# Cutting eight output stores by partitions: half-row stores of the first column half in two or three transfers each

## The chip, the cores and the metric

The kernel runs on one core of a Trainium2 chip. The metric is the device time of one execution in microseconds. The kernel before takes 368.6 us, the median of two runs (367.9 and 369.3).

## The reference, cut to what matters

Attention with a sigmoid in place of the softmax over 8 batches, 12 heads, 448 positions and head size 64; its output, as 3584 rows of 768 columns, goes through a soft mixture of experts with 8 experts of 4 slots each. All data is float32.

```python
attn = sigmoid(q @ k.T / sqrt(64) - log(448)) @ v        # per batch and head
x = attn.transpose(0, 2, 1, 3).reshape(3584, 768)
logits = x @ phi                                          # 3584 x 32
d = softmax over the 3584 rows;  slot_input = d.T @ x     # 32 x 768
h = relu(slot_input[e] @ w1[e]);  slot_out[e] = h @ w2[e] # w1: 768 x 1024, w2: 1024 x 768
c = softmax over the 32 slots;   out = c @ slot_out       # 3584 x 768
```

The weights w1 and w2 are 25 MB each, the output is 11 MB.

## The kernel before, in words

**Attention, to about 290 us.** Pairs of heads pass through TensorE (scores, then the product with v), with the sigmoid on ScalarE and the transposes on VectorE. Beside it SyncE loads q, k, v and the expert weights. The weights go into a ring of SBUF tiles (`ring_tile`, `load`, lines 116 to 173): a load waits until the tile's last reader is done, and the last weights of all are issued by SyncE between 296 and 313 us.

**Experts, to about 340 us.** `w1_part` and `h_part` (lines 716 to 736) work through w1, expert by expert. Then `w2_step` (lines 834 to 845) works through w2 in two column halves of 384 columns (`HALF`): the sixteen steps of half 0 first (lines 861 to 866), then the sixteen steps of half 1 (lines 870 to 880). Each step waits for the weights that it multiplies. `spread_sum` makes the 128-row operand `st` of one half, from which the output tiles of that half can be made.

**Output.** An output tile is 128 rows by 384 columns: `out_tile` (lines 787 to 790) is one matmul of the combine weights with `st` and one copy from PSUM to SBUF, on ScalarE for even tiles and VectorE for odd ones. `out_half(m, hf)` (lines 792 to 797) makes two such tiles, of row blocks m and m+1 and column half hf, side by side in one SBUF tile, and stores them in one transfer of 384 KB: each of the 128 partitions holds two runs of 384 floats (1536 bytes), which go to two rows of the output, 128 rows apart.

The order of the stores, all of them issued by SyncE, is fixed by the program. Eight calls of `out_half(m, 0)`, for m = 0, 2, ..., 14, stand between the w2 steps of half 1, one after each of the steps 4 to 11 (lines 879 and 880). After the last w2 step and its `spread_sum` come two stores of whole rows of one row block (`out_rows`, lines 882 and 883, 384 KB each), three of whole rows of two, four and four row blocks (`out_many`, lines 885 to 887, 768, 1536 and 1536 KB), and last the eight stores `out_half(m, 1)` (lines 889 and 890). The prediction calls the first eight the first-half stores, and the last eight the second-half stores.

Every engine executes its instructions in the order in which they are written (the program fixes the schedule of all five). SyncE's instructions from 296 us on are DMA issues alone: the last weight loads, then the stores. Ahead of each issue stands a wait for the data and for a DMA semaphore. The tile framework hands out the DMA semaphores by itself; the code names none.

Of the kernel before, what the change touches and what calls it, by code (L numbers as in the profile page):

```python
# [18 lines left out]
P = 128  # L19
# [10 lines left out]
HALF = DM // 2  # L30
# [26 lines left out]
ROWS = 128  # L57
NG = B * S // ROWS
NH = 16
LAG_T = 3  # L60
C4W = NBK * 4 * NSLOT
NR = 2
# [8 lines left out]
def soft_moe_attention(ctx: ExitStack, tc: tile.TileContext, qk, v, vl, first, phi, w, wq, w8, wz, cst, out):  # L71
    nc = tc.nc
# [43 lines left out]
    def ring_tile(size=1):  # L116
        while state["used"] + size > state["room"]:
            pool, n, used, room = slots[state["ring"]]
            state.update(ring=state["ring"] + 1, used=used, room=room)
            if pool == "wa":  # L120
                pool = wpa.tile([P, room * UNIT], F32, name=f"wa{n}")
            state["tile"] = pool
        t = state["tile"][:, state["used"] * UNIT:(state["used"] + size) * UNIT]
        state["used"] += size
        return t
# [67 lines left out]
    with ExitStack() as actx:  # L193
# [377 lines left out]
        for r in range(NP // 2):  # L571
            p = 2 * r
# [184 lines left out]
    def combine_split(n):  # L757
        lt, k = pieces[n][:2]
        c4 = wc_last[:, n % 3 * C4W:(n % 3 + 1) * C4W].rearrange("p (k a z s) -> p k a z s", k=NBK, a=2, z=2)
        nc.vector.tensor_copy(c4[:, 0:k, 0, 0, :], lt)  # L760
        nc.vector.tensor_tensor(
            out=c4[:, 0:k, 0, 1, :], in0=lt, in1=c4[:, 0:k, 0, 0, :].bitcast(F32), op=ALU.subtract)
        nc.scalar.copy(c4[:, 0:k, 1, :, :], c4[:, 0:k, 0, :, :].bitcast(F32))
        return c4

    def combine_turn(n, c4):
        pt = pt_tile()
        _, k, t0, nt = pieces[n]
        for c in range(k):
            w = min(P, nt - c * P)  # L770
            nc.tensor.transpose(
                out=pt[:, c * P:c * P + w], in_=c4[0:w, c].rearrange("p a z s -> p (a z s)").bitcast(F32),
                identity=csb[0:w, 0:w])
        at0 = t0
        while at0 < t0 + nt:
            i, m = divmod(at0, UNIT)
            w = min(UNIT - m, t0 + nt - at0)
            if m == 0:
                cts[i] = big[:, i * UNIT:(i + 1) * UNIT]
            nc.scalar.copy(cts[i][:, m:m + w], pt[:, at0 - t0:at0 - t0 + w])  # L780
            at0 += w
# [5 lines left out]
    def out_tile(ov, m, hf, k, t=0, n=1):  # L787
        pf = ps_t.tile([P, 512], F32, name="pt") if k % 2 else av_tile("av0")
        nc.tensor.matmul(pf[:, 0:HALF], ct_of(m, t, n), sts[hf], start=True, stop=True)  # L789
        (nc.scalar.copy, nc.vector.tensor_copy)[k % 2](ov, pf[:, 0:HALF])  # L790

    def out_half(m, hf):
        ov = ring_tile().rearrange("p (j c) -> p j c", j=2)
        for j in range(2):
            out_tile(ov[:, j, :], m + j, hf, j)
        nc.sync.dma_start(
            out[m * ROWS:(m + 2) * ROWS, hf * HALF:(hf + 1) * HALF].rearrange("(j p) c -> p j c", p=P), ov)

    def out_rows(m):
        ov = ring_tile().rearrange("p (j c) -> p j c", j=2)  # L800
        for hf in range(2):
            out_tile(ov[:, hf, :], m, hf, hf)
        nc.sync.dma_start(out[m * ROWS:(m + 1) * ROWS, :].rearrange("p (j c) -> p j c", j=2), ov)
# [10 lines left out]
    def gather(po):  # L814
        so = sb2.tile([P, HALF], F32, name="tmp")
        nc.scalar.copy(so[:], po[:, 0:HALF])
        return so

    def spread_sum(so, cuts=(0, HALF)):
        if sts:  # L820
            st = wc_last[:, 0:HALF]
        else:
            st = sb2.tile([P, HALF], F32R, name="st")[:]
        parts = list(zip(cuts, cuts[1:]))
        prs = [ps_t.tile([P, 512], F32, name="pt") if k else av_tile("av1") for k in range(len(parts))]
        for pr, (c0, c1) in zip(prs, parts):
            nc.tensor.matmul(pr[:, 0:c1 - c0], rep, so[:, c0:c1], start=True, stop=True)
        for pr, (c0, c1) in zip(prs, parts):
            (nc.scalar.copy if len(parts) > 1 else nc.vector.tensor_copy)(st[:, c0:c1], pr[:, 0:c1 - c0])
            nc.vector.tensor_tensor(  # L830
                out=st[64:128, c0:c1], in0=pr[64:128, 0:c1 - c0], in1=st[64:128, c0:c1].bitcast(F32), op=ALU.subtract)
        sts.append(st)

    def w2_step(po, hf, n):
        e, g = divmod(n, 2)
        h = hw[e % 2]
        if g == 0:
            o = NSLOT - SPE
            nc.gpsimd.tensor_copy(
                h[:, o:o + NFC * NSLOT].rearrange("p (f s) -> p f s", f=NFC)[:, :, 0:SPE], hc[:, e])  # L840
        for fl in range(4):
            k = (4 * g + fl) * NSLOT + NSLOT - SPE - SPE * e
            nc.tensor.matmul(  # L843
                po[32 * fl:32 * fl + 32, 0:HALF], h[:, k:k + NSLOT], w2_chunk(hf, e, g, fl),
                start=(n == 0), stop=(n == 2 * E - 1))
# [15 lines left out]
    for e in range(E):  # L861
        w2_step(po, 0, 2 * e)
        w2_step(po, 0, 2 * e + 1)
        if e >= LAG_T:
            combine_turn(e - LAG_T, c4s[e - LAG_T])
        c4s[e] = combine_split(e)
# [3 lines left out]
    for n in range(2 * E):  # L870
        w2_step(po, 1, n)
        if n == 1:
            spread_sum(so)
        if n < LAG_T:
            combine_turn(E - LAG_T + n, c4s[E - LAG_T + n])
            if n == LAG_T - 1:
                sctx.close()
                ps_t = ctx.enter_context(tc.tile_pool(name="ps_t", bufs=4, space=PSUM, reuse_waits="tile"))
        if 4 <= n < 4 + NH // 2:
            out_half(2 * (n - 4), 0)  # L880
    spread_sum(gather(po), (0, HALF // 2, HALF))
    for m in range(NH, NH + NR):
        out_rows(m)
    m = NH + NR
    for n in MANY:
        out_many(m, n)
        m += n
    assert m == NG
    for m in range(0, NH, 2):
        out_half(m, 1)  # L890
# [51 lines left out]
```

## Time and profile before

| | |
|---|---|
| median of two runs | 368.6 us |
| the profiled execution's own time | 368.86 us |
| its span, first to last instruction | 367.0 us |
| TensorE busy | 346.7 us, 94% of the span |
| VectorE, ScalarE, GpSimd busy | 66%, 61%, 3% |
| mean granted TensorE clock | 0.987 |
| bytes moved by DMA | 95.21 MB, mean 259 GB/s |
| output stores | 384 KB x18, 768 KB x1, 1536 KB x2 |

The shares are means over the whole span. The profile also cuts the span in 40 slices of 9.2 us and gives for each how busy an engine was and how many GB/s the DMA engines moved; the last slices are the ones in which the output is stored. The DMA share is the mean over the core's 16 DMA engines of the time that their packets took; since packets overlap a little it can stand some per cent above 1.

### The profile page before, as it was taken

Reading aid. Unit: us, or ns where it says so; the run is one execution under the profiler, and the core shown is the slowest. Engines: PE = TensorE matmul, PEld = TensorE weight load, DVE = VectorE, ACT = ScalarE, POOL = GpSimd, SP = SyncE. Lnnn points to the kernel's source line nnn. Section 1 sums busy time; section 2 is a strip of 40 time slices with the busy share of each in tenths; the row PEclk is TensorE's granted clock in tenths of the full one; section 3 lists DMA queues with packets and bytes.
Section 4 is the critical chain, followed back from the end, with each engine's and each line's share of the span. In section 5 each row is a group of like instructions: output and inputs, shape, how many; then the busy total and the mean of one; then the engine's idle time right before and its main releaser. Section 6 shows DMA issues by size and latency. Waiting matters only on the chain.

```text
span 367.0 us, 10400 instructions
## 1 busy us (share of the span) xinstructions
PE 346.7 (94%) x4341; PEld 158.7 (43%) x4341; DVE 242.7 (66%) x621; ACT 222.2 (61%) x307; POOL 10.1 (3%) x45
## 2 busy tenths in 40 slices
PE   9999999999999999999999999999999999897840
PEld 5333333544444446444444644464446554332620
DVE  0148829797795886859948695878956676232650
ACT  4777777677777774777777387747583123432640
POOL 1000000000000000000000000010003001000000
PEclk9999999999999999999999999999999999999995
DMA  7566666565677663666576378829989999999998
GB/s 256 184 219 197 200 225 189 174 210 160 229 227 212 200 197 110 212 198 211 196 230 187 121 256 262 283 59 372 318 300 332 421 436 425 415 422 406 399 419 305
DMA packets 34639, 95.21 MB, mean 259 GB/s; under 512 B 3616, under 2 KB 17184, under 8 KB 33184
## 3 DMA queue, kind: packets, MB, share of 16 engines
q1 hardware_dynamic: 34016, 92.58, 71.5%
q10 hardware_dynamic: 576, 1.97, 1.5%
q8 instruction: 34, 0.56, 0.6%
q14 instruction: 13, 0.11, 0.1%
HBM read 83.53 MB, written 11.01 MB: 258 GB/s over the span
## 4 chain that ended last, share of the span: by engine, by line
PE 85%; DMA 9%; DVE 2%; ACT 0%; issue 0%; ACTq 0%; DVEq 0%
PE sc L282 35%; PE av L327 34%; DMA wpe<-in_wq_dram 9%; PE av L189 6%; PE sc L449 3%; PE sc L387 2%; DVE wa L790 1%; PE av L789 1%; PE av L843 1%; PE sc L369 1%; PE av L567 1%; PE pt L789 1%; PE av L302 1%; PE av L449 0%; PE av L282 0%
## 5 line engine op out<-in xcount | busy, mean ns | idle before, releaser
L294 ACT ACTIVATE big<-sc,sm 128x896 f32<-128x896 f32 x167 | 167.7, 1007 | 77.2 <-PE sc L282 74.2
L327 PE MATMUL av<-big 64*64 64x448 f32 x1260 | 146.7, 536 | 0.0
L282 PE MATMUL sc<-big 64*64 64x448 f32 x896 | 111.3, 537 | 0.0
L327 PEld LDWEIGHTS av<-big 64*64 64x64 f32 x1260 | 47.5, 133 | 71.2 <-issue 68.9
L351 DVE STREAM_TRANSPOSE wa<-wpe 32x384 f32<-32x384 f32 (+5 forms) x144 | 58.0, 403 | 2.2
L282 PEld LDWEIGHTS sc<-big 64*64 64x64 f32 x896 | 35.5, 133 | 49.7 <-issue 39.9
L282 PE MATMUL sc<-wk 64*64 64x448 f32 x420 | 55.8, 537 | 0.0
L351 DVE STREAM_TRANSPOSE wa<-xy 32x192 f32<-32x192 f32 (+3 forms) x96 | 33.1, 345 | 1.6
L334 DVE TENSOR_TENSOR wpe<-wpe,av 128x448 f32<-128x448 f32 x18 | 11.2, 621 | 31.8 <-PE av L327 20.5
L282 PEld LDWEIGHTS sc<-wk 64*64 64x64 f32 x420 | 17.4, 133 | 22.3 <-issue 19.2
L351 DVE STREAM_TRANSPOSE wa<-wpx 32x288 f32<-32x288 f32 (+1 forms) x48 | 25.0, 520 | 0.8
L843 PE MATMUL av<-wa,hw 128*32 128x384 f32 x208 | 20.3, 493 | 2.7 <-DMA wa<-in_w_dram 1.6
L334 DVE TENSOR_TENSOR wpx<-wpx,av 128x448 f32<-128x448 f32 x15 | 9.3, 621 | 18.3 <-PE av L327 16.0
L189 PE MATMUL av<-wa,phi 128*32 128x256 f32 x312 | 18.2, 381 | 0.6 <-DVE phi L531 0.4
L790 DVE COPY wa<-pt 128x384 f32<-128x384 f32 x23 | 11.8, 554 | 4.5 <-PE pt L789 4.1
L790 ACT COPY wa<-av 128x384 f32<-128x384 f32 x23 | 10.7, 481 | 5.9 <-PE av L789 5.3
L334 DVE TENSOR_TENSOR xy<-xy,av 128x448 f32<-128x448 f32 x14 | 8.7, 621 | 8.3 <-ACT xy L330 6.6
L189 PEld LDWEIGHTS av<-wa,phi 128*32 128x32 f32 x312 | 9.6, 110 | 8.0 <-DVE phi L531 0.8
L736 ACT COPY t<-tmp 128x32 f32<-128x32 f32 x8 | 1.7, 218 | 18.3 <-DVE tmp L734 13.6
L351 DVE STREAM_TRANSPOSE wpe<-xy 32x256 f32<-32x256 f32 (+3 forms) x32 | 11.0, 345 | 0.5
L351 DVE STREAM_TRANSPOSE wpy<-wpx 32x288 f32<-32x288 f32 (+3 forms) x22 | 9.3, 424 | 0.4
L330 ACT COPY wpe<-av 128x448 f32<-128x448 f32 x18 | 9.4, 524 | 0.0
(191 smaller groups left out, 281.9 us busy)
## 6 DMA issues: line engine op xcount, KB each, us to landing
wa<-in_w_dram SPq DMA_DIRECT2D x52, 384.0 KB, 4.1
big<-in_qk_dram SPq DMA_DIRECT2D x32, 448.0 KB, 3.6
wa<-in_wq_dram SPq DMA_DIRECT2D x6, 1536.0 KB, 29.1
wa<-in_w_dram SPq DMA_DIRECT2D x3, 3072.0 KB, 20.8
big<-in_v_dram SPq DMA_DIRECT2D x45, 192.0 KB, 2.5
wk<-in_qk_dram SPq DMA_DIRECT2D x15, 448.0 KB, 3.3
out_dram<-wa SPq DMA_DIRECT2D x13, 384.0 KB, 7.4
out_dram<-wa SPq DMA_DIRECT2D x2, 1536.0 KB, 7.5
```

The costliest lines, as they stand in the source:

```text
L189: nc.tensor.matmul(ph[32 * j:32 * j + 32, 0:256], phi_sb[:, kc, :], wt, start=(kc == 0), stop=(kc == NKC - 1))
L282: nc.tensor.matmul(sc[h][64 * t:64 * t + 64, 0:S], qkts[pt][r, S + k0:S + k0 + 64], qkts[pt][r, 0:S], start=True, stop=True)
L294: nc.scalar.activation(att, tile2[:, :, 0:S], AF.Sigmoid, bias=nbias, scale=QSCALE)
L327: nc.tensor.matmul(o[t][r, 0:S], w, att[row, h, :], start=start, stop=stop)
L330: nc.scalar.copy(x_of(p), avs[p][1][:, 0:S])
L334: nc.vector.tensor_tensor(out=x_of(p), in0=x_of(p), in1=av[0][:, 0:S], op=ALU.add)
L351: nc.vector.transpose(y[32 * g:32 * g + 32, k0:k0 + n, c0:c0 + m, BLK * a:BLK * a + BLK], src)
L387: nc.tensor.matmul(lg[32 * j:32 * j + 32, BLK * c0[j]:BLK * (c0[j] + n)], phi_sb[:, hp, :], blocks(x, j if x is xa else (j + 2) % 4, n), s ...
L449: nc.tensor.matmul(sls[t][32 * a:32 * a + 32, BLK * k0:BLK * k1], zt[:, c * BLK:(c + 1) * BLK], y_of(t, gi, c)[:, k0:k1, BLK * a:BLK * a + ...
L789: nc.tensor.matmul(pf[:, 0:HALF], ct_of(m, t, n), sts[hf], start=True, stop=True)
L790: (nc.scalar.copy, nc.vector.tensor_copy)[k % 2](ov, pf[:, 0:HALF])
L843: nc.tensor.matmul(po[32 * fl:32 * fl + 32, 0:HALF], h[:, k:k + NSLOT], w2_chunk(hf, e, g, fl), start=(n == 0), stop=(n == 2 * E - 1))
```

## The change

`out_half` cuts its store along the partitions. A table gives the cuts for the first-half stores; a store that is not in the table goes out in one transfer as before. The tiles, the copies that fill them, the bytes stored and the order of the stores stay the same. Twelve transfers are added: the eight first-half stores become twenty.

```diff
+CUTS = {
+    (0, 0): (0, 120, 125, P), (2, 0): (0, 120, 127, P), (4, 0): (0, 120, 126, P), (6, 0): (0, 120, 124, P),
+    (8, 0): (0, 98, P), (10, 0): (0, 104, P), (12, 0): (0, 72, P), (14, 0): (0, 88, P)}
@@ out_half
-        nc.sync.dma_start(
-            out[m * ROWS:(m + 2) * ROWS, hf * HALF:(hf + 1) * HALF].rearrange("(j p) c -> p j c", p=P), ov)
+        rows = out[m * ROWS:(m + 2) * ROWS, hf * HALF:(hf + 1) * HALF].rearrange("(j p) c -> p j c", p=P)
+        cuts = CUTS.get((m, hf), (0, P))
+        for a, b in zip(cuts, cuts[1:]):
+            nc.sync.dma_start(rows[a:b], ov[a:b])
```

The pieces, in partitions, are 120+5+3, 120+7+1, 120+6+2, 120+4+4, 98+30, 104+24, 72+56 and 88+40.

## Rows read from the trace of the kernel before

**Rows 1.** The page: span, and DMA share (tenths) and rate in 40 slices.
```profile
span 367.0 us, 10400 instructions
...
DMA  7566666565677663666576378829989999999998
GB/s 256 184 219 197 200 225 189 174 210 160 229 227 212 200 197 110 212 198 211 196 230 187 121 256 262 283 59 372 318 300 332 421 436 425 415 422 406 399 419 305
```
**Rows 2.** The chain of waits from 300 us on: start, duration, what.
```profile
305.72 33.14 DMA wpe<-in_wq_dram
...
351.75 2.10 DVE wa L790 x4
```
**Rows 3.** Stretches: busy us (and count) of PE, PEld, DVE, ACT, POOL, PEclk, DMA share, GB/s.
```profile
339.00:344.00 5.00, 3.72 (x26) 2.13 (x26) 1.35 (x4) 1.99 (x6) 0.00 (x0) 1.00 1.07 397
344.00:347.00 3.00, 2.96 (x11) 2.69 (x12) 2.86 (x6) 2.48 (x6) 0.00 (x0) 1.00 1.03 392
347.00:350.00 3.00, 3.00 (x13) 2.40 (x12) 2.78 (x6) 2.62 (x6) 0.00 (x0) 1.00 1.06 438
...
354.00:364.00 10.00, 0.00 (x0) 0.00 (x0) 0.00 (x0) 0.00 (x0) 0.00 (x0) 0.67 1.02 390
364.00:365.00 1.00, 0.00 (x0) 0.00 (x0) 0.00 (x0) 0.00 (x0) 0.00 (x0) 0.50 0.99 364
365.00:365.50 0.50, 0.00 (x0) 0.00 (x0) 0.00 (x0) 0.00 (x0) 0.00 (x0) 0.50 0.26 95
```
**Rows 4.** SyncE's DMA issues in order of time: start, first to last end, what, count.
```profile
296.05 4.32 SPq L171 DMA_DIRECT2D wa<-in_wq_dram  x4
300.87 5.17 SPq L171 DMA_DIRECT2D wpe<-in_wq_dram  x2
313.03 0.33 SPq L139 DMA_DIRECT2D wpx<-in_wz_dram  x1
326.65 0.40 SPq L796 DMA_DIRECT2D out_dram<-wpx  x1
327.97 8.13 SPq L796 DMA_DIRECT2D out_dram<-wpy  x4
337.05 3.05 SPq L796 DMA_DIRECT2D out_dram<-wa  x3
343.97 1.12 SPq L803 DMA_DIRECT2D out_dram<-wa  x2
```
**Rows 5.** SyncE's waits, 326 to 367 us: total, times, longest.
```profile
SPq L938 <- DMA out_dram<-wa: 5.0, 1, 5.0
...
SPq L803 <- DVE wa L790: 3.8, 1, 3.8
SPq L796 <- DMA wa<-in_wq_dram: 3.0, 2, 1.7
SPq L796 <- DMA wpe<-in_wq_dram: 2.3, 2, 1.4
```
**Rows 6.** The load issued at 298.6: issue ns, start, us to landing.
```profile
L171 SPq DMA_DIRECT2D wa<-in_wq_dram x1: 328/328/328, 298.6 to 298.6; - x1
...
DMA to landing us min/median/max: 32.7/32.7/32.7
```
**Rows 7.** SyncE's issue of the fourth first-half store: start, duration.
```profile
331.45 2.38 SPq L796 DMA_DIRECT2D out_dram<-wpy  x1
```
**Rows 8.** The first of the first-half stores: issue ns, start, us to landing.
```profile
L796 SPq DMA_DIRECT2D out_dram<-wpx x1: 399/399/399, 326.6 to 326.6; - x1
...
DMA to landing us min/median/max: 13.7/13.7/13.7
```
**Rows 9.** The last of the first-half stores: issue ns, start, us to landing.
```profile
L796 SPq DMA_DIRECT2D out_dram<-wa x1: 643/643/643, 339.5 to 339.5; - x1
...
DMA to landing us min/median/max: 7.7/7.7/7.7
```
**Rows 10.** The page's DMA issues, the smallest of many: count, KB each, us to landing.
```profile
big<-in_vl_dram SPq DMA_DIRECT2D x23, 64.0 KB, 2.0
```

## The prediction, made before the changed kernel ran

> **What bounds the kernel now.** The stores belong to the last tenth of the span, so I read the page's slices first, then the chain of waits from 300 us on, then short stretches of the tail, then SyncE's own queue. In the slices the DMA share stands at nine tenths or more from about 290 us to the end, at 400 to 436 GB/s [rows 1]: the last weights and then the output go through full DMA engines. The chain says the same of the weights: 33.14 us of it are one load, issued at 305.72 and landed at 338.86 [rows 2]. After that the chain runs through the copies, which end at 351.75 + 2.10 = 353.85 us [rows 2]; it follows engines and does not see that the stores go on for 12 us after the last copy. The stretches do: from 354 to 364 no engine computes and the DMA share is 1.02 [rows 3]. SyncE's wait for the last store is its longest in this time, 5.0 us [rows 5].
>
> So the end is set by how long the DMA engines need for their bytes once the weights are in. What matters is the slowest of the sixteen. The share is 0.99 in 364 to 365 and 0.26 in the half microsecond after it [rows 3]: all sixteen run dry within about 1 us of each other. None is a straggler that would gain from a smaller part, and none has more than some half microsecond of room for a larger one.
>
> SyncE's queue holds a second limit. The fourth first-half store is issued at 331.45 [rows 7], just when a load issued at 298.6 lands, 298.6 + 32.7 = 331.3 [rows 6]. Counted through the issues, that load is the eighth transfer before it [rows 4]. Four first-half stores wait for a load in this way [rows 5]. I read it as eight DMA semaphores in rotation: a transfer goes out when the eighth one before it has landed.
>
> **The change, part by part.** Bytes, tiles, copies and matmuls stay. Three things change: how the first-half stores lie on the sixteen DMA engines, how many transfers pass through SyncE, and which landing each waits for.
>
> *The load of the engines.* A whole half-row store is 128 partitions, 8 for each of 16 engines. Its price comes from the stretch that holds nothing but such stores: 393,216 bytes at 390 GB/s [rows 3] are 1.01 us, so one partition costs the engine that carries it 0.126 us. No row shows a transfer of other than 128 partitions, so I bound the new distribution. One end: the pieces spread as evenly as before, and no engine gets more; 0 us. The other end: a piece is cut into equal shares of whole partitions, on as many engines as divide it, always from the same first engine on. Then that engine carries 8+1+1, 8+1+1, 8+1+1, 8+1+1, 7+2, 8+2, 6+4 and 8+4 partitions, 81 in place of 64: 17 x 0.126 = 2.14 us more. The sixteenth carries none of the eight stores and is 64 x 0.126 = 8.1 us ahead, which helps nobody, as every later store again needs all sixteen. I take the second end, because equal shares are the nearest to the one thing that is seen, sixteen engines that end together [rows 3]. A row shows no engine's number, so whether the first engines are the early or the late ones within that 1 us is open: 2.14 less up to 1 is the lower end of this case.
>
> The Trainium skill, page "DMA: Bandwidth & Descriptors", section "Why a DMA increments its semaphore by 16 and not by 1", states such a rule: the number of engines is the largest one up to 16 that divides the partitions, and they are the lowest-numbered. No run here shows it yet; by it the count is the same 81.
>
> *Twelve more issues.* An issue takes 0.40 us where nothing holds it [rows 8], so twelve are 4.8 us of SyncE. Nothing that is computed waits for SyncE here. Between the eighth first-half store, out at 337.05 + 3.05 = 340.10, and the first whole-row store at 343.97 [rows 4] it waits 3.8 us for VectorE's copy [rows 5], and it waits ahead of that too. The issues alone cost 0; without that cover they would cost 4.8.
>
> *The eight semaphores.* This is the added wait. Before, all eight stores were out at 340.1 us. After, the first eight transfers are only stores 1 and 2 and two pieces of store 3; pieces 4 to 8 wait for the loads for which stores 4 to 8 waited, so the eighth piece goes out at about 339.5. The ninth waits for the first piece, which lands where the first store did, at 326.6 + 13.7 = 340.3 [rows 8]. Pieces 9 to 16 leave as 1 to 8 land, until about 343. A transfer needs at least some 2.0 us from issue to landing [rows 10], so pieces 17 to 20 and the whole-row stores behind them go out from about 345 on: the first whole-row store is piece 21 and leaves between 345 and 347.5 in place of 343.97. What hides this is the engines' backlog: before, the last first-half store landed at 339.5 + 7.7 = 347.2 [rows 9], and on the engine with 81 partitions that becomes 349.3. The engine that sets the end thus still has work when the late store arrives. Ends: 0 (fully covered) and 3.5 us (the whole delay is idle time of the slowest engine). I take 0.3, near the covered end, because the backlog of 347.2 lies so close to 347.5.
>
> *Sum.* 2.14 + 0 + 0.3 = 2.4 us on the profiled execution's 368.86 gives 371.3. The median of the runs is 0.26 below that execution; I give **371.2 us**, 0.7% slower, which counts as no change: about 2%, 7.4 us, is what a measurement of this kernel can tell from none.
>
> **The rivals.**
>
> *Pieces of part of the partitions move more slowly* (slower). The price above assumes that an engine moves its partitions at the usual rate whichever they are. If the engines that share a piece get into each other's way at the SBUF side, each of the eight stores takes longer. At half the rate they take 8 x 1.01 = 8.1 us more, 368.86 + 2.14 + 8.1 = 379; at two thirds of the rate 4 us more, 375. It decides, that is passes 2%, from about 5 us on, 0.65 us a store. For it: all traffic here is at 390 to 438 GB/s whatever is moved [rows 3], as if something common limits it. Against it: the engines read the pieces out of step, since a piece waits in each engine's queue behind other work. The Trainium skill, page "SBUF — State Buffer", section "Door 1: The DMA port swizzle (why [64,N] ≈ [32,N])", speaks for it: 64 partitions in a row reach half of the 16 ports and get about half the bandwidth. By it the first part of 72+56 or 88+40, more than half of which lies in the lower 64 partitions, would be slow. No run here shows it.
>
> *Nothing happens* (no change). The pieces spread evenly all the same, or the first engines are ahead by as much as they get. Then only covered issues are added: 368.2 to 369.8. For it: between 344 and 347 the rate falls to 392 from the 438 of the next stretch [rows 3], so some engines have idle time there. At (438 - 392)/438 of 3 us that is 0.3 us each on average, too little for 2.14. That the change does not do what it says, because pieces land on all sixteen engines, is this case too.
>
> *A small gain.* The engines relieved are the late ones, and those loaded have room. The ends lie within 1 us [rows 3], so the gain is at most half of that and the 0.3 us above: 0.8, or 367.8 us. Against it: the 17 extra partitions alone are twice the whole spread.
>
> **How the numbers follow.** Chances: the forecast, 369.8 to 373, 0.53; slower pieces, 373 to 380, 0.21, of which half is above 376; nothing happens, 0.20; a small gain, 0.06. For the range I leave out the gain and the part of the second case above 376.5: 368.2 to 376.5. Faster by over 2% would need 361.2 us, which no case reaches, so 0.01 for what I have not thought of; slower by over 2% gets the upper half of the slow case, 0.11; within 2% the remaining 0.88.
>
> **What would show it.** Right: in the last 2 to 3 us before the last landing the DMA share falls in steps well below 1, as lightly loaded engines finish first; the first whole-row store leaves at 345 to 347.5 us; and SyncE's waits ahead of the cut stores and of the first whole-row store now name stores. If the sixteen still end within 1 us, the shares are not as I count them. If the rate of 339 to 344 us stands far below 397 GB/s [rows 3] while many engines have work, the slow pieces are at work. The prediction is wrong if the stores' queue is kept empty by the semaphores for several microseconds, or if the weights' last landing, at 338.86 [rows 2], moves.

## The result, and the profile after

The changed kernel takes 373.86 us, the median of two runs (373.59 and 374.12), against 368.6 us before: the ratio is 1.0138 with a 95% interval of 1.0113 to 1.0163, so 4.2 to 6.0 us slower. The forecast was 371.2 us in a range of 368.2 to 376.5. The sign and the range held; the loss is twice the forecast 2.6 us, and it lies where the prediction had put one of its rivals (373 to 380).

The page first: the span is 4.8 us longer than before.

```profile
span 371.8 us, 10412 instructions
...
DMA packets 34705, 95.21 MB, mean 256 GB/s; under 512 B 3682, under 2 KB 17250, under 8 KB 33250
```

The same line of the page before:

```profile
DMA packets 34639, 95.21 MB, mean 259 GB/s; under 512 B 3616, under 2 KB 17184, under 8 KB 33184
```

The bytes are the same. The packets under 512 B are 3682 where the page before has 3616. They count the engines that a transfer uses, one small packet for each: 3616 is 226 x 16, one for each of 16 engines of 226 transfers. The eight whole stores had 8 x 16 = 128. Equal whole shares of the pieces (15+5+3, 15+7+1, and so on) make 193; the piece of one partition, which holds two runs, can go on two engines and makes it 194. 194 - 128 = 66 is the measured difference. So the pieces do leave engines out, as the prediction took it, and no piece of 120 is on sixteen engines.

The weights' last landing, in the chain of waits (start, duration, what), is where it was, 338.67 for 338.86 [rows 2]:

```profile
305.51 33.16 DMA wpe<-in_wq_dram
```

The stretches (columns as in [rows 3]) show where the time went:

```profile
339.00:344.00 5.00, 3.68 (x27) 2.12 (x20) 1.54 (x4) 2.18 (x6) 0.00 (x0) 1.00 0.80 234
344.00:347.00 3.00, 3.00 (x12) 2.75 (x12) 2.84 (x7) 2.49 (x6) 0.00 (x0) 1.00 0.79 232
347.00:350.00 3.00, 3.00 (x13) 2.41 (x13) 2.85 (x6) 2.52 (x7) 0.00 (x0) 1.00 0.74 218
350.00:354.00 4.00, 3.07 (x13) 1.61 (x12) 3.67 (x8) 3.05 (x7) 0.00 (x0) 1.00 1.03 399
...
364.00:368.00 4.00, 0.00 (x0) 0.00 (x0) 0.00 (x0) 0.00 (x0) 0.00 (x0) 0.50 1.04 369
...
369.00:370.00 1.00, 0.00 (x0) 0.00 (x0) 0.00 (x0) 0.00 (x0) 0.00 (x0) 0.50 0.99 353
370.00:371.00 1.00, 0.00 (x0) 0.00 (x0) 0.00 (x0) 0.00 (x0) 0.00 (x0) 0.50 0.23 83
```

Between 339 and 350 us the DMA engines move 234, 232 and 218 GB/s where they moved 397, 392 and 438 [rows 3]. That is (163 x 5 + 160 x 3 + 220 x 3) KB = 1.96 MB that is missing at 350 us, 4.9 us at 400 GB/s: as much as the whole loss. Two things make up the low rate. The share is 0.74 to 0.80, so engines stand idle a fifth to a quarter of the time. And a busy engine moves less: 234/0.80 = 293 GB/s for each full share, against 397/1.07 = 371 before. From 350 us on the engines are full again, and they end together: 0.99, then 0.23. The steps at the end that the prediction asked for are not there.

The trace's records of single packets (one run of bytes that one engine moves) size both. The half-row runs are packets of 1536 bytes. Of those that begin between 339 and 350 us the median takes 65 ns in both kernels, but 350 of 1632 take 100 ns or more in the changed kernel, 4 of 1709 before. Per engine, what packets take beyond the median of their size in the kernel before adds up to 1.8 us, against 0.1, and the packets keep an engine busy for 8.6 us, against 11.4 (more than the 11 us of the stretch, because packets overlap). So of the 4.9 us some 2.8 us are idle time and some 1.7 us are slow packets: a fifth of the packets are much slower, not all of them a little.

SyncE's issues in order of time (columns as in [rows 4]) and three of its waits (as in [rows 5]):

```profile
327.97 1.07 SPq L802 DMA_DIRECT2D out_dram<-wpx  x3
331.25 11.77 SPq L802 DMA_DIRECT2D out_dram<-wpy  x11
343.14 4.50 SPq L802 DMA_DIRECT2D out_dram<-wa  x6
347.74 1.92 SPq L808 DMA_DIRECT2D out_dram<-wa  x2
349.76 3.33 SPq L815 DMA_DIRECT2D out_dram<-wa  x3
```

```profile
SPq L802 <- DMA wpe<-in_wq_dram: 2.8, 2, 1.6
SPq L802 <- ACT wa L793: 2.0, 4, 0.8
SPq L802 <- DMA out_dram<-wpx: 0.7, 1, 0.7
```

The first whole-row store (L808) leaves at 347.74 in place of 343.97 [rows 4]. Only 0.7 us of this is a wait for a store. The rest is issuing: the trace has the eighth piece out at 339.47 and the ninth issued at 340.20, and from there SyncE issues twelve pieces one behind the other, 7.5 us or 0.63 us each, until 347.7. (The 2.0 us that the view puts down to ScalarE's copies are no wait for data: the copies of all eight first-half stores had ended by 337.2 us.) The twelve hold 642 partitions, 1.97 MB, so SyncE hands out some 260 GB/s, less than the 390 that the engines move [rows 3]; that is how they run empty.

### The profile page after: what moved, and what is told of

It reads as the page before. It is cut to its first block, busy times and chain, and to the rows that moved or that the text cites. A ratio compares the mean times of both kernels' runs of the same rounds, so it can differ in the third digit from the quotient of the medians.

```text
span 371.8 us, 10412 instructions
## 1 busy us (share of the span) xinstructions
PE 347.1 (93%) x4341; PEld 160.9 (43%) x4341; DVE 242.7 (65%) x621; ACT 222.2 (60%) x307; POOL 10.1 (3%) x45
## 2 busy tenths in 40 slices
DMA packets 34705, 95.21 MB, mean 256 GB/s; under 512 B 3682, under 2 KB 17250, under 8 KB 33250
## 3 DMA queue, kind: packets, MB, share of 16 engines
q10 hardware_dynamic: 576, 1.97, 1.4%
## 4 chain that ended last, share of the span: by engine, by line
PE 82%; DMA 10%; DVE 2%; ACT 1%; issue 0%; SPq 0%; ACTq 0%; DVEq 0%
PE sc L285 34%; PE av L330 33%; DMA wpe<-in_wq_dram 9%; PE av L192 6%; PE sc L452 2%; PE sc L390 2%; PE av L848 1%; DVE wa L793 1%; DMA xy<-in_first_dram 1%; PE av L792 1%; PE sc L372 1%; PE av L305 1%; PE pt L792 1%; PE av L452 0%; PE av L285 0%
## 5 line engine op out<-in xcount | busy, mean ns | idle before, releaser
L330 PEld LDWEIGHTS av<-big 64*64 64x64 f32 x1260 | 48.3, 133 | 70.5 <-issue 68.2
L783 ACT CAST big<-sc 128x512 fp32r<-128x512 f32 (+5 forms) x11 | 4.5, 433 | 9.2 <-PE sc L774 9.2
```

Of the source, the lines that this page charges most:

```text
L330: nc.tensor.matmul(o[t][r, 0:S], w, att[row, h, :], start=start, stop=stop)
```

## The experiments

Three theories were put to the test. A, late issue: eight pieces are out when the weights have landed, and the other twelve then cost SyncE so long that the engines run dry. B, uneven engines: the engine with 81 partitions in place of 64 sets the end. C, slow pieces: engines that read part of the partitions hold each other up.

**The same twenty transfers, cut by columns.**

```diff
-        cuts = CUTS.get((m, hf), (0, P))
-        for a, b in zip(cuts, cuts[1:]):
-            nc.sync.dma_start(rows[a:b], ov[a:b])
+        cols = ((0, 0, HALF), (1, 0, HALF // 2), (1, HALF // 2, HALF)) if m < 8 else ((0, 0, HALF), (1, 0, HALF))
...
+            for j, c0, c1 in cols:
+                nc.sync.dma_start(rows[:, j, c0:c1], ov[:, j, c0:c1])
```

> The twenty first-half transfers stay, but each piece holds all 128 partitions: the stores are cut by columns (one row block whole, the other whole or in two pieces of 192 columns). Every engine then carries the same load. Theory A, late issue (the eight semaphores hold the pieces back until the weights have landed, and SyncE then needs until about 347 us to issue them, so the first whole-row store is late and the engines run dry): first whole-row store issued at 346.5 to 348.5 us, total 371.5 to 374. Theory B, uneven engines (the engine with 81 partitions in place of 64 sets the end): no cost, 368.3 to 369.3. Theory C, slow pieces (engines that read part of the partitions hold each other up): no cost either, and the rate between 339 and 344 us stays near 397 GB/s.

Measured: 371.94 against 369.5 us, ratio 1.0066 (1.0040 to 1.0091), 2.4 us. Its first whole-row store and its stretches:

```profile
347.22 0.89 SPq L811 DMA_DIRECT2D out_dram<-wa  x2
```

```profile
339.00:344.00 5.00, 2.91 (x23) 1.68 (x24) 0.68 (x2) 1.50 (x4) 0.00 (x0) 1.00 0.87 295
344.00:347.00 3.00, 2.95 (x13) 2.40 (x11) 2.76 (x6) 2.31 (x6) 0.00 (x0) 1.00 0.98 347
347.00:350.00 3.00, 3.00 (x12) 2.83 (x12) 2.85 (x6) 2.48 (x6) 0.00 (x0) 1.00 1.03 385
```

Every engine carries the same load and every transfer reads all partitions, and nearly half of the loss is there, with the store as late as A expected and a share of 0.87. A is at work, and it is not the whole. The rate that the expectation gave for C, near 397 GB/s, missed: the engines starve here too.

**The same twenty transfers in multiples of 16 partitions.**

```diff
-    (0, 0): (0, 120, 125, P), ...
+    (0, 0): (0, 96, 112, P), (2, 0): (0, 96, 112, P), (4, 0): (0, 96, 112, P), (6, 0): (0, 96, 112, P),
+    (8, 0): (0, 96, P), (10, 0): (0, 96, P), (12, 0): (0, 64, P), (14, 0): (0, 80, P)}
```

> Twenty pieces by partitions as in the changed kernel, but of multiples of 16: 96+16+16 four times, 96+32 twice, 64+64, 80+48. By equal shares each of the 16 engines then carries 8 partitions of every store. Theory A, late issue: as in the changed kernel, 372.5 to 374.5, first whole-row store at 347 to 348.5 us. Theory B, uneven engines: no cost, 368.3 to 369.3. Theory C, slow pieces: between, 370 to 374, since the pieces still lie in part of the partitions; the rate from 339 to 350 us would be clearly below that of the cut by columns.

Measured: 373.2 us, ratio 1.0108 (1.0084 to 1.0133). The page's small packets and the stretches:

```profile
DMA packets 34831, 95.21 MB, mean 256 GB/s; under 512 B 3808, under 2 KB 17376, under 8 KB 33376
```

```profile
339.00:344.00 5.00, 3.68 (x22) 2.41 (x14) 2.26 (x6) 2.74 (x7) 0.00 (x0) 1.00 0.73 213
344.00:347.00 3.00, 3.00 (x12) 2.71 (x12) 2.83 (x6) 2.50 (x6) 0.00 (x0) 1.00 0.91 269
```

3808 - 3616 = 192 = 12 x 16: all engines take part in every piece, so the loads are even. Still the kernel loses 0.42% more than with the cut by columns, about 1.6 us (the two intervals together leave +-0.36%). The total fits theory A (372.5 to 374.5) as well as C (370 to 374); what tells them apart is the rate. A full share moves 213/0.73 = 292 GB/s, against 295/0.87 = 339 with the columns, and 349 of 1632 half-row packets between 339 and 350 us take 100 ns or more, against 4 of 1496. So pieces of part of the partitions are slower here, and unevenness is not needed for it. The 1.6 us are not slowness alone: the engines also stand idle longer than with the columns (share 0.73 and 0.91 for 0.87 and 0.98), and the issue of the ninth piece alone, at 339.25, took SyncE 1.76 us.

**Only the first piece of each store.**

```diff
-        for a, b in zip(cuts, cuts[1:]):
-            nc.sync.dma_start(rows[a:b], ov[a:b])
+        nc.sync.dma_start(rows[0:cuts[1]], ov[0:cuts[1]])
```

> Only the first piece of each first-half store goes out (120, 120, 120, 120, 98, 104, 72 and 88 partitions), so the other 182 of 1024 partitions of these stores are left out and the number of transfers is that of the kernel before. Left out are 559 KB, 1.4 us at 400 GB/s. Theory A, late issue: no delay, first whole-row store at 344 us, total 366.8 to 368.6. Theory B, uneven engines: the busiest engine carries 61 in place of 64 partitions, about 0.4 us less, 368.0 to 368.6. Theory C, slow pieces: the rate from 339 to 344 us stays below 320 GB/s and the total rises above 369.5 although bytes are missing.

Measured: 370.04 against 369.5 us, ratio 1.0020 (1.0000 to 1.0039), although 1.4 us of bytes are missing. A alone and B alone had this faster. It speaks for C, but weakly. The limit given for C, 369.5, is what the kernel before itself took beside it. The rate between 339 and 344 us, 347 GB/s, was not below the 320 that C asked for. And not all of the 1.4 us can be counted as lost: the kernel with pieces of 96 (below) leaves out 786 KB, 2.0 us, and its one run is only 0.7 us faster than the kernel before. In the trace 79 of 1629 half-row packets between 339 and 350 us take 100 ns or more, and the first whole-row store leaves at 344.97, 1.0 us late, with a share of 0.81 from 344 to 347 us.

**The twelve smaller pieces issued later.**

```diff
...
+        rest.extend((rows[a:b], ov[a:b]) for a, b in zip(cuts[1:], cuts[2:]))
...
     for n in MANY:
         out_many(m, n)
+        for _ in range(4):
+            nc.sync.dma_start(*rest.popleft())
```

> All twenty pieces of the changed kernel, but the twelve smaller ones are issued later, four behind each of the three stores of several row blocks, where SyncE waits for copies. The load of each engine stays as in the changed kernel (81 partitions of these stores on the busiest). Theory A, late issue: the first whole-row store leaves at 344 us again and most of the loss is gone, 368.5 to 370.5. Theory B, uneven engines: the loss of the busiest engine stays, 370.7 or more. Theory C, slow pieces: the first pieces still move slowly, 371 to 374.

Measured: 374.41 us, ratio 1.0147 (1.0117 to 1.0178). SyncE's issues, the small pieces on L895, and the stretch from 354 to 364 us:

```profile
344.03 1.15 SPq L810 DMA_DIRECT2D out_dram<-wa  x2
345.41 0.86 SPq L817 DMA_DIRECT2D out_dram<-wa  x1
346.32 1.81 SPq L895 DMA_DIRECT2D out_dram<-wpx  x2
348.17 1.30 SPq L895 DMA_DIRECT2D out_dram<-wpy  x2
349.60 0.36 SPq L817 DMA_DIRECT2D out_dram<-wa  x1
350.01 3.02 SPq L895 DMA_DIRECT2D out_dram<-wpy  x4
353.14 1.03 SPq L817 DMA_DIRECT2D out_dram<-wa  x1
354.22 0.49 SPq L895 DMA_DIRECT2D out_dram<-wpy  x1
354.75 3.89 SPq L895 DMA_DIRECT2D out_dram<-wa  x3
358.75 8.97 SPq L803 DMA_DIRECT2D out_dram<-wa  x8
```

```profile
354.00:364.00 10.00, 0.00 (x0) 0.00 (x0) 0.00 (x0) 0.00 (x0) 0.00 (x0) 0.64 0.94 304
```

The first whole-row store leaves at 344.03 again, and the loss stays: the forecast of A, 368.5 to 370.5, fell. The twelve small pieces take SyncE 1.81 + 1.30 + 3.02 + 0.49 + 3.89 = 10.5 us, 0.88 us each, although several of them hold 1 to 7 partitions. The second-half stores, which began at 350.40 before, begin at 358.75, and from 354 to 364 us the engines run at 304 GB/s in place of 390 [rows 3]. The delay was only moved: twelve more issues cost what they cost wherever SyncE's issues set the pace. But the share in that stretch is still 0.94, so idle time is the smaller part of it there; 142 of its 954 half-row packets take 100 ns or more, and the slow packets have moved with the small pieces.

**One engine's extra load, and its control.**

```diff
             out_half(2 * (n - 4), 0)
+    nc.sync.dma_start(phi_sb.rearrange("p k s -> p (k s)")[0:59, 0:192], w[0][0:59, 0:192])
```

The control has 64 and 177 in place of 59 and 192.

> The kernel before, its stores uncut, with one extra transfer behind the eighth first-half store: a load of 59 partitions by 768 bytes into a tile that is no longer read, 45 KB, which leaves the result as it is. By equal whole shares 59 (a prime) can lie on one engine only: 59 packets, about 2.2 us if one of 768 bytes takes 36 to 37 ns as in the cut by columns. That is the size of the 17 partitions that the changed kernel puts on its busiest engine. Theory B, uneven engines: the end moves by 1.2 to 2.3 us, 370.0 to 371.8. If the engines' idle time hides such a load, it moves by less than 0.7 us.

> The control of the one above: the extra load has 64 partitions by 708 bytes, the same 45 KB, 4 partitions on each of 16 engines, about 0.15 us each. All theories: 0 to 0.4 us over the kernel before. A larger loss would be the price of one more transfer in itself.

Measured: 369.3 us and 369.2 us against 368.72; ratios 1.0014 (0.9997 to 1.0030) and 1.0015 (1.0000 to 1.0031). The page's packets, of the one and of the control:

```profile
DMA packets 34699, 95.26 MB, mean 259 GB/s; under 512 B 3617, under 2 KB 17244, under 8 KB 33244
```

```profile
DMA packets 34719, 95.26 MB, mean 259 GB/s; under 512 B 3632, under 2 KB 17264, under 8 KB 33264
```

3617 is one more than 3616: the 59 partitions were on one engine (by the prediction's count the first; the trace gives no engine's number), and 3632 is 16 more. Both cost the same, at most 0.3%. Two microseconds on this engine cost nothing beyond one more transfer: the price on which B rests is refuted for it. The trace shows why. The load's 59 packets, the only ones of 768 bytes in this time, ran from 344.97 to 346.92 us, and it landed at 347.38. So this engine had its part of the eighth store behind it at 344.97, while the last of the sixteen landed that store at 347.11: some 1.7 us ahead, if a landing comes 0.46 us after the last packet, as for the load. In the middle of the tail the engines are not in step. The semaphores of the kernel before say the same: the sixteen landings of its eighth first-half store lie between 344.58 and 347.12 us, 2.5 us, and those of its last store within 0.9 us.

**Eight transfers in halves of the partitions, and their control.**

```diff
+    def out_pair(m):
+        ov = ring_tile(2).rearrange("p (j c) -> p j c", j=4)
+        ...
+        for a, b in zip(PAIR, PAIR[1:]):
+            nc.sync.dma_start(rows[a:b], ov[a:b])
```

`PAIR` is (0, 64, P), in the control (0, P); stores 2 to 7 are made as three such pairs.

> Eight first-half transfers as in the kernel before, with the same bytes and with 8 partitions' worth of every store on each engine: stores 2 and 3, 4 and 5, 6 and 7 are made as pairs in one tile, and each pair goes out in two transfers, one of the partitions 0 to 63 and one of 64 to 127. Neither the number of transfers nor the load of the engines changes. Theory A, late issue, and theory B, uneven engines: within 0.7 us of the pairs in whole transfers. Theory C, slow pieces: 1.5 to 5 us above them, and the rate from 339 to 344 us well below 397 GB/s.

> The control of the pairs in halves: stores 2 and 3, 4 and 5, 6 and 7 go out as pairs, each pair one transfer of 128 partitions and 768 KB, five first-half transfers in all. Bytes and loads as before. Theory A, late issue: as the kernel before or a little faster, 367.8 to 369.5, since all first-half stores are out earlier. Theories B and C: as the kernel before.

Measured: 370.19 us, ratio 1.0038 (1.0021 to 1.0055), and 369.61 us, ratio 1.0015 (0.9998 to 1.0032). The stretch of the halves:

```profile
339.00:344.00 5.00, 2.82 (x22) 1.59 (x23) 0.68 (x2) 1.50 (x4) 0.00 (x0) 1.00 1.06 391
```

The halves are 0.23% or 0.85 us above the whole pairs, less than the 1.5 us that C asked for and not clear of the two intervals, which together leave +-0.24%, and they move at 391/1.06 = 369 GB/s per full share. Half of the partitions in a transfer does not slow the engines by itself when both halves are in the queue. The whole pairs, the one version that took transfers away, gain nothing.

**Half of the change each.** One kernel keeps the cuts of the last four stores, the other those of the first four.

```diff
-CUTS = { ... }
+CUTS = {(8, 0): (0, 98, P), (10, 0): (0, 104, P), (12, 0): (0, 72, P), (14, 0): (0, 88, P)}
```

> Only the last four first-half stores are cut (98+30, 104+24, 72+56, 88+40), the first four go out whole: twelve first-half transfers in place of eight or twenty. Theory A, late issue: four more transfers hold little back; first whole-row store at 344 to 345.5 us; alone 368.7 to 370. Theory C, slow pieces: these are the pieces that moved slowly when only the first pieces went out, so most of the slow-piece loss is here: 1.5 to 3 us over the kernel before, 370.2 to 371.7, and under 320 GB/s per full DMA share between 342 and 348 us.

> Only the first four first-half stores are cut (120+5+3, 120+7+1, 120+6+2, 120+4+4), the last four go out whole: sixteen transfers. Theory A, late issue: the four whole stores and the last piece behind the twelve pieces wait for the landing of pieces, so the first whole-row store leaves at 345 to 347 us: 1 to 2.5 us over the kernel before, 369.7 to 371.2. Theory C, slow pieces: the pieces of 120 moved at the full rate when they went out alone, so little is added: 368.7 to 370. If both parts act on their own, the losses of this kernel and of the last four add up to about 5 us.

Measured: 371.66 us, ratio 1.0069 (1.0044 to 1.0095), for the last four; 371.95 us, ratio 1.0072 (1.0053 to 1.0091), for the first four. First whole-row store and stretches of the last four:

```profile
344.57 1.95 SPq L806 DMA_DIRECT2D out_dram<-wa  x2
```

```profile
339.00:344.00 5.00, 3.67 (x27) 2.11 (x26) 1.44 (x4) 2.08 (x6) 0.00 (x0) 1.00 0.92 325
344.00:347.00 3.00, 3.00 (x11) 2.75 (x12) 2.83 (x7) 2.48 (x6) 0.00 (x0) 1.00 0.82 251
```

and of the first four:

```profile
345.55 2.05 SPq L806 DMA_DIRECT2D out_dram<-wa  x2
```

```profile
339.00:344.00 5.00, 3.69 (x26) 2.12 (x26) 1.37 (x4) 2.01 (x6) 0.00 (x0) 1.00 0.85 276
344.00:347.00 3.00, 2.98 (x11) 2.73 (x12) 2.84 (x6) 2.48 (x6) 0.00 (x0) 1.00 1.04 365
```

0.69% and 0.72% add up to 1.41%, against 1.38% for the whole change: within intervals that together leave +-0.3% the losses add up. They are not of one kind. With the last four cut the store is 0.6 us late only, and the loss comes with 251/0.82 = 306 GB/s per full share (C had asked for under 320 between 342 and 348 us; 342 to 345 gives 244/0.82 = 298, 345 to 348 gives 307/0.87 = 353). With the first four cut the store is 1.6 us late and the share falls to 0.85 between 339 and 344 us; 276/0.85 = 325 shows that some slowness is in it as well, against the expectation for C, and the loss of 0.72%, 2.7 us, is a little above the 1 to 2.5 us that A gave.

**One size of piece throughout.**

```diff
+        n = 96 if hf == 0 else P
...
+        nc.sync.dma_start(rows[0:n], ov[0:n])
```

The other kernel has 120.

> Each of the eight first-half stores carries the partitions 0 to 95 only, in one transfer: a quarter of their bytes, 786 KB, is left out. No pieces are added and all 16 engines carry 6 partitions. It is run for its rate. Theory C with slowness by an odd share per engine (6 partitions, not 4 or 8): under 330 GB/s per full DMA share between 339 and 344 us. Theory C with slowness only where engines are left out or pieces are many: 365 to 375 GB/s per full share, as before.

> Each of the eight first-half stores carries the partitions 0 to 119 only, in one transfer: a sixteenth of their bytes, 197 KB, is left out. By equal whole shares 15 engines carry 8 partitions each and the last one none. Theory C with slowness by an odd share per engine: 365 to 375 GB/s per full share between 339 and 344 us. Theory C with slowness wherever an engine is left out: under 350.

Each ran once (368.84 and 369.5 us), for its rate:

```profile
339.00:344.00 5.00, 3.17 (x24) 1.94 (x25) 0.79 (x3) 1.50 (x4) 0.00 (x0) 1.00 0.98 355
```

```profile
339.00:344.00 5.00, 3.06 (x24) 1.80 (x25) 0.69 (x2) 1.50 (x4) 0.00 (x0) 1.00 1.00 373
```

355/0.98 = 362 and 373/1.00 = 373 GB/s per full share: neither 6 partitions an engine nor an engine left out is slow by itself. That leaves C without its mechanism. The packets say where the slowness is. Of the half-row packets between 339 and 350 us the share that takes 100 ns or more is 21% in the changed kernel and with the multiples of 16, 7% with the last four and 7% with the first four cut, 5% with the first pieces only, 3% with the halves, and under 2% in the kernel before, with the columns, the whole pairs, the pieces of 96 and those of 120. The slow kernels have pieces of different shares one behind the other; which resource they meet in was not settled.

## Why the prediction was right or wrong

**Right: the bound, the new distribution and eight transfers in flight.** The DMA engines set the end, the weights did not move, and no computing engine was touched. The pieces leave engines out exactly as counted (66 small packets more). The rule of the Trainium skill, page "DMA: Bandwidth & Descriptors", section "Why a DMA increments its semaphore by 16 and not by 1", agrees with the trace to the packet: 66 here, 192 for the multiples of 16, 1 for 59 partitions. Eight transfers in flight held too: the eighth piece went out at 339.47 for a forecast of about 339.5, and the ninth at 340.20 for 340.3. The first whole-row store, at 347.74, came just past the forecast 345 to 347.5, but for another reason: the forecast let pieces 10 to 20 wait for landings, and the trace has them wait for SyncE's issues.

**Wrong: "I take 0.3, near the covered end".** This is the step that failed. The engine with 81 partitions was to have work until 349.3, so that a late store found it busy. The engines had run dry long before: the share is 0.80 from 339 us on, because the same eight semaphores and SyncE's pace held back the first-half pieces themselves, not only the stores behind them. That is nearly the prediction's own sign of being wrong, a queue kept empty for several microseconds. The cut by columns, which has this term almost alone, measures it at 2.4 us (1.5 to 3.4). The term's upper end, 3.5, held there.

**Wrong: "the issues alone cost 0".** They were to fit into SyncE's wait for VectorE. The semaphores push twelve of them behind 340.2 us, and there they are dense and cost 0.63 us each (0.88 with the pieces moved later), not the 0.40 of one that stands alone [rows 8]. 7.5 us do not fit into 3.8.

**Mis-sized: 2.14 us for the busiest engine.** Two microseconds on the first engine measure 0 beyond the control. I had read the spread of the engines where they end, 1 us, as their spread throughout; in the middle it is 2.5 us, and the loaded engine was some 1.7 us ahead of the last. (The stretch from 354 to 364 us does not hold only half-row stores, as I took it: the last store of four row blocks lands at 358.18. From 360 to 364 us the rate is 387 GB/s, so the price of a partition stands.) The rival in which the first engines are ahead by what they get was right on this point. What unevenness costs on the other engines is the difference of the change and the even multiples of 16, 0.30%, less than the +-0.35% of the two intervals: not resolved. Engines that get less gain nothing, as was said. No steps show at the end, because the gaps close along the whole stores that follow: the sixteen landings of the first whole-row store lie 1.2 us apart, those of the last store 0.7 us.

**The slower rival was half right.** Pieces are slower (293 GB/s per full share for 371). The multiples of 16 lose about 1.6 us more than the columns, part of it idle time, and the slow packets of the changed kernel make 1.7 us per engine by 350 us. The mechanism is not shown. By the Trainium skill's page "SBUF — State Buffer", section "Door 1: The DMA port swizzle (why [64,N] ≈ [32,N])", transfers of 64 partitions in a row would get about half the bandwidth; the halves moved at 391 GB/s, and for halves that stand one behind the other in the queue the measurement decides against it.

Together: twenty transfers of all partitions lose 2.4 us by late issue, pieces in multiples of 16 some 1.6 us more, and 1.1 us that the intervals do not resolve make the measured 5.1 us. The forecast's sum of 2.4 us (on 368.6 it makes 371.0; the 371.2 given is 0.16 too high) came from a term that costs nothing where it was tried, 2.14, and from one that was eight times too small. So the sign follows from the mechanism, but that the time lies in the range is in part luck: the range reached that far only because it took in half of the slower rival.

## What to carry to other kernels

Where a tail is bound by DMA and its transfers are spread evenly, cutting them buys nothing; count the transfers in flight first, because with eight semaphores in rotation twenty small transfers leave less in the queue than eight large ones, and price an issue by its pace in a dense row of the same transfers, not by one that stands alone. A backlog that hides a late transfer must be counted after the change, with the new transfers in it. Equal finishing times at the end say little about how far the DMA engines are apart in the middle.

## What the runs showed of the hardware that was not expected

A DMA issue on SyncE costs 0.40 us alone [rows 8] and 0.63 to 0.88 us in a dense row of pieces, hardly less for a piece of a few partitions. It is not one price for all transfers: in the kernel before the eight second-half stores, with two runs in each of 128 partitions, take 10.58 us in a dense row, 1.3 us each. What sets the pace was not tried.

```profile
350.40 10.58 SPq L796 DMA_DIRECT2D out_dram<-wa  x8
```

The same second-half stores, uncut in all kernels, moved at 387 GB/s in the kernel before, and at 369 GB/s from 364 to 368 us in the changed kernel. A stretch of the kernel before, and the last whole stretch of the cut by columns:

```profile
360.00:364.00 4.00, 0.00 (x0) 0.00 (x0) 0.00 (x0) 0.00 (x0) 0.00 (x0) 0.50 1.05 387
```

```profile
364.00:366.00 2.00, 0.00 (x0) 0.00 (x0) 0.00 (x0) 0.00 (x0) 0.00 (x0) 0.50 1.03 368
```

For eight stores, 3.15 MB, that is 8.5 in place of 8.1 us, so 0.4 us of the loss in these two kernels. In the cut by columns the engines had come into step by running dry together: the sixteen landings of a store lie 0.2 us apart. That the step is the cause is unlikely: the halves move at 369 GB/s from 360 to 364 us too, and there the landings lie almost 3 us apart. The cause stays open.
